# Block-sparse attention and an MLP mixer in one kernel: channel mixing paced over the next batch's attention, gates of the later pairs in fp16 parts

## The chip, the cores and the metric

One core of a Trainium2 chip runs the whole kernel. Five engines work at the same time, each through its own list of instructions in order, and semaphores tie the lists together: TensorE (PE in the profile; its weight loads are PEld), VectorE (DVE), ScalarE (ACT), GpSimd (POOL) and SyncE (SP, which issues transfers here). Matmuls write to PSUM, which is small and is handed out in tiles. The metric is device time in microseconds (us).

## The reference

Inputs are q, k and v of shape (4 batches, 8 heads, 768 positions, 64 wide) and four weight matrices, all float32. The first half is attention in which each query sees only some blocks of 64 keys:

```python
k_rep = k.reshape(B, H, n_blocks, block, D).mean(axis=3)
gate_scores = np.einsum('bhsd,bhnd->bhsn', q, k_rep)
causal = pos[:, None] // block >= np.arange(n_blocks)[None, :]
gate_scores = np.where(causal, gate_scores, -1000000000.0)
top_idx = np.argsort(gate_scores, axis=-1)[..., -top_k:]      # top_k = 3
# a query sees its 3 best blocks and its own, and no later position
scores = scale * np.matmul(q, k.transpose(0, 1, 3, 2))
...
return np.matmul(attn, v).astype(np.float32)
```

The second half takes the attention's output as x (4, 768, 512), mixes over positions and then over channels:

```python
xt = x.transpose(0, 2, 1)
h = np.maximum(xt @ w_tok1, 0.0) @ w_tok2        # 768 -> 256 -> 768
u = x + h.transpose(0, 2, 1)
h2 = np.maximum(u @ w_ch1, 0.0) @ w_ch2          # 512 -> 1536 -> 512
return (u + h2).astype(np.float32)
```

## The kernel before

**Work.** Two heads of one batch make a pair; there are 16 pairs, 4 to a batch, and pair i belongs to batch i // 4. For each pair the kernel

- loads k and q (SyncE) and turns them with fp32 transposes into PSUM (`transposes`, L333), copies them out in fp32 on ScalarE (`evac_t`, L342) and casts each head's half to fp16 on GpSimd (`cast`, L348, into the tiles KA and Q);
- makes the gates: sums each key block (`ksum`, L356), places the two heads' sums in a small fp32 matrix (`kcopy`, L364), multiplies with q in fp32 (`gate`, L374: five matmuls of 24 columns, each recorded as two), adds the causal bias (`gm`, L382), takes the best eight of 12 (`top`, L391), compares with the third (`below`, L398), turns it into a bias (`bias`, L406), transposes that (`mask`, L417) and copies it into spare rows of Q (`put_mask`, L425), so that the score matmul itself adds the block mask;
- computes the scores transposed (keys on the partitions) in three groups for each head (`scores`, L439), the exponential of each group (`expo`, L452), and sets the wrong half of the diagonal blocks to zero: for pair 0 by an added matmul with a triangle (L443, `i < TRI`), for the others by a multiplication on VectorE (`diag`, L458);
- multiplies with v (`av`, L468, 21 matmuls of 65 columns for a head, whose last column gives the sum) and normalises (`recip`, `norm`, L476 and L487).

Token mixing of a batch (`tok1`, `umix`, `uadd`) follows its four pairs; batch 0 does it in quarters as its pairs come. u is turned by TensorE for batch 0 (`utr`, `uput`) and through DRAM by SyncE for the others (`store_u`, `turn_u`). The first half of channel mixing is `ch1` (L580, 24 groups of four matmuls) with a relu after each (`relu2`: the 512-column groups on ScalarE, L590; the 256-column groups on VectorE, L592). The second half is a 2x2-block product done with seven block products instead of eight (`prod`, L644), in three rounds j, each with four operand sums on VectorE (`hsum`), three copies out of PSUM on ScalarE (`keep`, L652), and output sums on VectorE and GpSimd (`vsum`, `oput`, `vu` L666, `psum` L684, `osum` L689).

**Order.** `plan` (L69) sets the order of all instructions before the program is built. Every step is an `Op` with an engine, an assumed duration, the steps it needs, a priority (low goes first) and the buffers it takes; for each engine `plan` takes, among the steps that could start within 60 ns of the earliest one, that of the lowest priority. The priorities are due times: pair i's scores have 10 i and up, its preparation 10 (i - 1) (10 (i - 2.5) for the first four). Batch b's channel mixing has 1000 (b + 1) and up, token mixing of batches 1 to 3 has 960 less: with these, channel mixing goes only where no attention can. Buffers come in rings (`RINGS`): two PSUM tiles `big` of two banks for transposes and scores, three single banks `bank` for gates, masks, token and channel mixing; once all scores are done, channel mixing may take `big` as well.

**Start.** Sixty matmuls on zeros keep TensorE running until the first data is there (`dummy`, L710). The weights are loaded by GpSimd's queue, each after a given cast (`WAIT`).

Of the kernel before, what the change touches and what calls it, by code (L numbers as in the profile page):

```python
# [31 lines left out]
TRI = 1  # L32
EARLY = 1
UVIA = 1
LEAD = 960.0
WARM, COLD, WARM_END = 120, 20, 17000.0
IDLE = 1e9
WAIT = [("kt", 3, 1), ("kt", 3, 1), ("qt", 3, 1), ("qt", 3, 1), ("qt", 4, 1), ("qt", 4, 1),
# [3 lines left out]
class Op:  # L42


    __slots__ = ("eng", "occ", "rec", "deps", "prio", "fn", "takes", "start", "size", "both")

    def __init__(self, eng, occ, rec, deps, prio, fn, takes=(), size=0):
        self.eng, self.occ, self.rec, self.prio, self.fn = eng, occ, rec, prio, fn
        self.deps = [d for d in deps if d is not None]
        self.takes = takes  # L50
        self.size = size
        self.start = None
        self.both = False

# [14 lines left out]
def plan(ops, rings, near=60.0):  # L69
# [10 lines left out]
    for op in ops:  # L80
        n = 0
        for d in op.deps:
            users.setdefault(id(d), []).append(op)
            n += 1
        waiting[id(op)] = n
        if n == 0:
            ready[op.eng].append(op)
# [16 lines left out]
    while left:  # L104
# [7 lines left out]
        for e, cand in ready.items():  # L112
# [7 lines left out]
            for op in cand:  # L120
                t = free[e]
                for d in op.deps:
                    t = max(t, finish(d, e))
                if op.both:
                    t = max(t, free["POOL"]) if t >= pool_from else t
                elif e == "POOL" and both_from <= t < both_to:
                    t = both_to
                ok = True
                for buf in op.takes:
# [10 lines left out]
                    buf.slot = first[1:]  # L140
                if ok:
                    lst.append((t, op))
            if not lst:
                continue
            t0 = min(t for t, _ in lst)
            pick = min((x for x in lst if x[0] <= t0 + near), key=lambda x: (x[1].prio, x[0]))
# [3 lines left out]
        t, op = best  # L150
# [30 lines left out]
        ready[op.eng].remove(op)  # L181
        order.append(op)
        left -= 1
        for u in users.get(id(op), []):
            waiting[id(u)] -= 1
            if waiting[id(u)] == 0:
                ready[u.eng].append(u)
# [4 lines left out]
def kernel(  # L192
# [20 lines left out]
    scale = 1.0 / (D ** 0.5)  # L213
    MASKV = -30000.0
# [8 lines left out]
    RINGS = dict(big=2, bank=3, av=1, ql=3, kl=3, v32=2, qt=2, kt=2, gs=2, e0=3, e1=3, e2=3, rc=2,  # L223
                 x16=2, h1=1, u=2, uT=2, h2=1, ob=3, s1=2, s3=2, s4=1, f32=6)
# [24 lines left out]
    ks2 = [sp.tile([128, 2 * NB], FP, tag=f"ks{r}", name=f"ks{r}") for r in range(R)]  # L249
    bn16 = [sp.tile([128, NJ, 2, 64], F16, tag=f"bn{r}", name=f"bn{r}") for r in range(2)]  # L250
# [22 lines left out]
    def act(cols, deps, prio, fn, takes=()):  # L273
        return op("ACT", 70 + cols * 0.833, 173 + cols * 0.833, deps, prio, fn, takes)

# [60 lines left out]
    def evac_t(t32, i):  # L336
        def f():
            name = "qt" if t32 == "ql" else "kt"
            t = sb(name, [128, S], FP, f"{name}_{i}")
            T[name, i] = t  # L340
            p = T["tr", t32, i]
            nc.scalar.copy(out=t, in_=p[:, 0:S])  # L342
        return f

    def cast(dst, name, i, x):
        def f():
            lo = 64 * x
            nc.gpsimd.tensor_copy(out=dst[i % R][x][lo:lo + 64, :], in_=T[name, i][lo:lo + 64, :])  # L348
        return f
# [9 lines left out]
    def kcopy(i):  # L359
        def f():  # L360
            kst = T["kst", i]
            r = i % R
            for lo, c in ((64, 0), (0, NB)):
                nc.vector.tensor_reduce(out=ks2[r][lo:lo + 64, c:c + NB],  # L364
                                        in_=kst[lo:lo + 64, :].rearrange("p (n o) -> p n o", o=1),
                                        axis=AX.X, op=ALU.add)
        return f

    def gate(i):
        def f():  # L370
            g = ps("bank", [128, GJ, 2 * NB], "gps")
            T["gps", i] = g
            for j in range(GJ):
                nc.tensor.matmul(out=g[:, j, :], lhsT=T["qt", i][:, 128 * j + 128:128 * j + 256],  # L374
                                 rhs=ks2[i % R], start=True, stop=True)
        return f

    def gm(i):
        def f():
            t = sp.tile([128, GJ, 2 * NB], FP, tag="gm", bufs=2, name=f"gm_{i}")  # L380
            T["gm", i] = t
            nc.vector.tensor_tensor(out=t, in0=T["gps", i], in1=gbias, op=ALU.add)  # L382
        return f

    def top(i):
        def f():
            t = sp.tile([128, GJ, 2, 8], FP, tag="m8", bufs=2, name=f"m8_{i}")
            T["m8", i] = t
            for j in range(GJ):
                for x in range(2):  # L390
                    nc.vector.max(out=t[:, j, x, :], in_=T["gm", i][:, j, NB * x:NB * x + NB])  # L391
        return f

    def below(i):
        def f():
            t = sp.tile([128, GJ, 2 * NB], FP, tag="lt", bufs=2, name=f"lt_{i}")
            T["lt", i] = t
            nc.vector.tensor_tensor(  # L398
                out=t.rearrange("p j (x n) -> p j x n", n=NB),
                in0=T["gm", i].rearrange("p j (x n) -> p j x n", n=NB),  # L400
                in1=T["m8", i][:, :, :, 2:3].broadcast_to([128, GJ, 2, NB]), op=ALU.is_lt)
        return f

    def bias(i):
        def f():
            nc.vector.scalar_tensor_tensor(  # L406
                out=bn16[i % 2][:, 1:NJ, :, 0:NB],
                in0=T["lt", i].rearrange("p j (x n) -> p j x n", n=NB), scalar=MASKV,
# [3 lines left out]
    def mask(i):  # L412
        def f():
            p = ps("bank", [128, 128 * GJ], "bps", F16)
            T["bps", i] = p
            for j in range(GJ):
                nc.tensor.transpose(out=p[:, 128 * j:128 * j + 128],  # L417
                                    in_=bn16[i % 2][:, j + 1, :, :].rearrange("p x n -> p (x n)"),
# [3 lines left out]
    def put_mask(i, x):  # L422
        def f():
            lo = 64 if x == 0 else 0
            nc.vector.tensor_copy(out=QA[i % R][x][lo:lo + NB, 128:S], in_=T["bps", i][lo:lo + NB, :])  # L425
# [65 lines left out]

    def tok1(b, t):
# [10 lines left out]
    def relu1(b, t):  # L503
        return lambda: nc.scalar.activation(out=T["h1", b][:, t, :], in_=T["tok1", b, t], func=AF.Relu)
# [29 lines left out]
    def relu1c(b, c):  # L534
        return lambda: nc.scalar.activation(out=T["h1", b][:, :, 128 * c:128 * c + 128], in_=T["tok1", b, c], func=AF.Relu)
# [29 lines left out]
    def uput(b, cc):  # L565
        def f():
            if cc == 0:
                T["uT", b] = sb("uT", [128, NCC, S], F16, f"uT_{b}")
            nc.vector.tensor_copy(out=T["uT", b][:, cc, :], in_=T["utps", b, cc])
# [14 lines left out]
    def relu2(b, fc, n):  # L584
        def f():
            a, e = CH[n]
            if fc == 0 and ("h2", b) not in T:
                T["h2", b] = sb("h2", [128, NFC, S], F16, f"h2_{b}")
            if n == 0:
                nc.scalar.activation(out=T["h2", b][:, fc, a:e], in_=T["c1", b, fc, n], func=AF.Relu)  # L590
            else:
                nc.vector.tensor_scalar(out=T["h2", b][:, fc, a:e], in0=T["c1", b, fc, n], scalar1=0.0,  # L592
                                        scalar2=None, op0=ALU.max)
        return f

    def ch2(b, j, part, lo, hi):
        def f():
            if part == 0:
                T["c2", b, j, lo] = ps("bank", [128, hi - lo], "c2")
            for fc in range(4 * part, 4 * part + 4):  # L600
                nc.tensor.matmul(out=T["c2", b, j, lo], lhsT=T["h2", b][:, fc, 128 * j:128 * j + 128],
                                 rhs=wc2_16[:, fc, lo:hi], start=(fc == 0), stop=(fc == NFC - 1))
# [11 lines left out]
    def halves(b, j):  # L614
        h2 = T["h2", b]
        c1, c2 = slice(128 * j, 128 * j + 128), slice(384 + 128 * j, 512 + 128 * j)
        return h2[:, 0:HF, c1], h2[:, HF:NFC, c1], h2[:, 0:HF, c2], h2[:, HF:NFC, c2]
# [30 lines left out]
    def keep(b, j, key):  # L648
        def f():
            t = sb("f32", [128, 256], FP, f"p{key}_{b}_{j}")  # L650
            T["p" + key, b, j] = t
            nc.scalar.copy(out=t, in_=T["c2" + key, b, j])  # L652
# [77 lines left out]
    for i in range(NP):  # L730
# [9 lines left out]
        for t32, src, off in (("kl", k, 0), ("ql", q, 0.1)):  # L740
# [5 lines left out]
            name = "kt" if t32 == "kl" else "qt"  # L746
            tb = Buf(name)
            if name == "kt" and i < EARLY:
                O["ksum", i] = dve(900, [O["tr", t32, i]], pre + 1, ksum(i))
                big.users.append(O["ksum", i])  # L750
            O[name, i] = act(768, [O["tr", t32, i]] + ([O["ksum", i]] if name == "kt" and i < EARLY else []),
                             pre + 0.5 + off, evac_t(t32, i), [tb])
            big.users.append(O[name, i])
            dst = KA if name == "kt" else QA
            for x in range(2):
                O["cast", name, i, x] = op("POOL", 880, 900, [O[name, i]] + zq + last_scores(x), pre + 4 + off,
                                           cast(dst, name, i, x))
                tb.users.append(O["cast", name, i, x])
            if name == "kt":
                if i >= EARLY:  # L760
                    O["ksum", i] = dve(870, [O["kt", i]], pre + 1, ksum(i))
                    tb.users.append(O["ksum", i])
                O["kcopy", i] = dve(200, [O["ksum", i], O.get(("gate", old))], pre + 1, kcopy(i))
            else:
                qb = tb
# [5 lines left out]
        O["gate", i] = pe(1120, [O["kcopy", i], O["qt", i]], pre + 2, gate(i), [gb])  # L771
        qb.users.append(O["gate", i])
        gs = Buf("gs")
        O["gm", i] = dve(200, [O["gate", i]], pre + 3, gm(i), [gs])
        gb.users.append(O["gm", i])
        O["top", i] = dve(720, [O["gm", i]], pre + 3, top(i))
        O["lt", i] = dve(200, [O["top", i]], pre + 3, below(i))
        O["bias", i] = dve(195, [O["lt", i], O.get(("mask", i - 2))], pre + 3, bias(i), both=True)
# [3 lines left out]
        for x in range(2):  # L782
            O["put", i, x] = dve(410, [O["mask", i]] + zq + last_scores(x), pre + 4, put_mask(i, x))
# [35 lines left out]
    for b in range(B):  # L819
        fill = 1000.0 * (b + 1)  # L820
        mix = fill - LEAD if b else fill
        early = -1.0
# [199 lines left out]
```

## Time and profile before

| | us |
|---|---|
| median of 3 runs (271.99 to 275.36) | 272.19 |
| the profiled execution | 271.2 |
| its span, first to last instruction | 269.4 |
| TensorE busy | 254.9 (95%) |
| VectorE busy | 187.1 (69%) |
| ScalarE busy | 155.1 (58%) |
| GpSimd busy | 129.3 (48%) |

Times inside the profile start at the span's beginning. "Busy" is the union of an engine's records; records of neighbouring instructions can overlap. A line number names the line of the kernel that issued an instruction, and line numbers of the changed kernel differ from those of the kernel before. In the profile's rows, `out<-in` gives the program's tile names without numbers, then the shapes, then how often; after the bar come busy us and the mean duration in ns. Two rows of operations that the change removes or moves, as the view of groups by shape gives them: the fp32 gate matmuls take 20.0 us of records (160 of them, mean 267 ns), the diagonal multiplication 18.3 us (30, mean 611 ns).

### The profile page before, as it was taken

The numbers are of one execution on the slowest core, as the hardware profiler recorded it, in microseconds if no ns is written. First come the engines' busy times: TensorE is split into PE (matmuls) and PEld (weight loads), VectorE is DVE, ScalarE is ACT, GpSimd is POOL, SyncE is SP. The second block draws the span as 40 slices with busy tenths as digits, with TensorE's granted clock in tenths as the row PEclk, the third lists the DMA queues.
The fourth block names the chain that finished last, engine by engine and source line by source line (L and its number), as shares of the span: only waits on it lengthen the run. The fifth ranks groups of instructions, "written<-read, shape, count | busy, mean of one in ns | idle before, by whom it ended". The sixth has DMA issues, their size and how long they took to land.

```text
span 269.4 us, 6752 instructions
## 1 busy us (share of the span) xinstructions
PE 254.9 (95%) x2640; PEld 198.3 (74%) x2640; DVE 187.1 (69%) x574; ACT 155.1 (58%) x224; POOL 129.3 (48%) x171
## 2 busy tenths in 40 slices
PE   8798889999998999999999999999999999999992
PEld 5687678887776878778788887656775558866881
DVE  4468768889799978659997974418953459544861
ACT  2357798697888788977678872442224432244220
POOL 8678907478418563544826155000890006910384
PEclk9999999999999999999999999999999999999998
DMA  8999999999999944747048213000581004920033
GB/s 174 199 210 226 170 208 226 207 220 192 231 205 229 195 102 98 157 102 135 2 136 100 82 42 116 2 0 0 195 213 62 2 0 157 230 86 2 0 119 117
DMA packets 94240, 34.69 MB, mean 129 GB/s; under 512 B 85568, under 2 KB 90584, under 8 KB 94208
## 3 DMA queue, kind: packets, MB, share of 16 engines
q1 hardware_dynamic: 90128, 29.89, 51.9%
q0 software_dynamic: 3360, 4.11, 9.0%
q8 instruction: 21, 0.34, 0.6%
q10 hardware_dynamic: 720, 0.25, 0.5%
q14 instruction: 11, 0.09, 0.1%
HBM read 27.17 MB, written 8.65 MB: 133 GB/s over the span
## 4 chain that ended last, share of the span: by engine, by line
PE 66%; DVE 17%; DMA 6%; POOL 5%; issue 2%; ACT 1%; SPq 1%; POOLq 0%; DVEq 0%; ACTq 0%
PE c L580 21%; PE c L644 14%; PE sps L439 9%; PE aps L468 5%; PE gps L374 5%; DMA ql<-in_q_dram 4%; PE tok L499 3%; DMA wc<-in_moe_w_ch_dram 3%; POOL vu L666 2%; PE tql L333 2%; DVE u L519 2%; DVE Q L425 2%; PE tkl L333 2%; DVE e L458 2%; PE ups L511 2%
## 5 line engine op out<-in xcount | busy, mean ns | idle before, releaser
L452 ACT ACTIVATE e<-sps 128x768 f16<-128x768 f32 (+2 forms) x96 | 85.4, 920 | 15.3 <-PE sps L439 14.1
L580 PE MATMUL c<-uT,wc 128*128 128x256 f16 (+1 forms) x384 | 66.8, 326 | 0.0
L580 PEld LDWEIGHTS <-wc 128*128 128x128 f16 x384 | 37.0, 98 | 22.5
L439 PE MATMUL sps<-Q,KA 128*128 128x128 f16 (+3 forms) x384 | 50.5, 259 | 2.6 <-ACT e L452 2.5
L666 POOL TENSOR_TENSOR vu<-v,u 128x256 f32<-128x256 f32 x36 | 28.6, 819 | 34.7 <-DVE v L659 34.3
L590 ACT ACTIVATE h<-c 128x512 f16<-128x512 f32 x48 | 28.7, 597 | 27.2 <-PE c L580 27.0
L592 DVE TENSOR_SCALAR h<-c 128x256 f16<-128x256 f32 x48 | 20.2, 421 | 31.8 <-PE c L580 31.6
L348 POOL CAST KA<-kt 64x768 f16<-64x768 f32 x32 | 27.0, 844 | 28.8 <-ACT kt L342 27.7
L439 PEld LDWEIGHTS <-KA 128*128 128x128 f16 x384 | 29.4, 100 | 14.4 <-issue 2.2
L348 POOL CAST Q<-qt 64x768 f16<-64x768 f32 x32 | 27.6, 862 | 9.8 <-ACT qt L342 8.5
L644 PEld LDWEIGHTS <-h 128*128 128x128 f16 x288 | 27.7, 98 | 5.1 <-DVE h L629 1.3
L684 POOL TENSOR_TENSOR pc<-pc,pd 128x256 f32<-128x256 f32 x12 | 9.1, 760 | 41.2 <-ACT pd L652 41.2
L468 PE MATMUL aps<-V,e 128*128 128x65 f16 x672 | 26.7, 193 | 0.2 <-ACT e L452 0.2
L468 PEld LDWEIGHTS <-e 128*128 128x128 f16 x672 | 25.2, 98 | 2.0 <-ACT e L452 0.3
L304 POOL CAST V<-v 128x768 f16<-128x768 f32 x16 | 14.6, 913 | 20.6 <-DMA v<-in_v_dram 17.3
L644 PEld LDWEIGHTS <-s 128*128 128x128 f16 x216 | 20.9, 98 | 2.9
L342 ACT COPY kt<-tkl 128x768 f32<-128x768 f32 x16 | 12.8, 800 | 16.2 <-PE tkl L333 9.9
L374 PEld LDWEIGHTS gps<-ks,qt 128*128 128x128 f32 x160 | 19.2, 192 | 2.9 <-DVE ks L364 1.1
L374 PE MATMUL gps<-ks,qt 128*128 128x24 f32 x160 | 20.0, 267 | 1.3 <-ACT qt L342 0.5
L458 DVE TENSOR_TENSOR e<-e,m 128x768 f16<-128x768 f16 x30 | 18.3, 611 | 3.0 <-ACT e L452 2.8
L644 PE MATMUL c<-t,h 128*128 128x256 f16 x144 | 19.4, 273 | 0.6 <-DVE h L629 0.6
L644 PE MATMUL c<-wc,h 128*128 128x256 f16 x144 | 19.6, 273 | 0.0
(73 smaller groups left out, 372.1 us busy)
## 6 DMA issues: line engine op xcount, KB each, us to landing
kl<-in_k_dram SPq DMA_DIRECT2D x32, 192.0 KB, 4.7
ql<-in_q_dram SPq DMA_DIRECT2D x32, 192.0 KB, 4.5
v<-in_v_dram SPq DMA_DIRECT2D x16, 384.0 KB, 5.4
out_dram<-ob SPq DMA_DIRECT2D x24, 256.0 KB, 2.3
wc<-in_moe_w_ch_dram POOLq DMA_DIRECT2D x8, 384.0 KB, 7.4
uscr<-u SPq DMA_DIRECT2D x3, 768.0 KB, 3.7
w<-in_moe_w_tok_dram POOLq DMA_DIRECT2D x2, 384.0 KB, 7.2
KA<-indc POOLq DMA_DIRECT2D x2, 72.0 KB, 4.6
```

What stands on the lines that cost most here:

```text
L304: nc.gpsimd.tensor_copy(out=V16[i % (R + 1)][:, :, :, 0:D], in_=T["v32", i])
L348: nc.gpsimd.tensor_copy(out=dst[i % R][x][lo:lo + 64, :], in_=T[name, i][lo:lo + 64, :])
L374: nc.tensor.matmul(out=g[:, j, :], lhsT=T["qt", i][:, 128 * j + 128:128 * j + 256], rhs=ks2[i % R], start=True, stop=True)
L439: nc.tensor.matmul(out=p[:, off + a:off + a + n], lhsT=KA[i % R][x][:, 128 * kk:128 * kk + 128], rhs=QA[i % R][x][:, q0 + a:q0 + a + n], s ...
L452: nc.scalar.activation(out=e[:, 0:width], in_=T["sps", i, x, g][:, 0:width], func=AF.Exp, scale=scale)
L458: nc.vector.tensor_tensor(out=d, in0=d, in1=m0.broadcast_to([128, NJ, 128]), op=ALU.mult)
L468: nc.tensor.matmul(out=p[:, jq, :], lhsT=T["e", i, x, g][:, o:o + 128], rhs=V16[i % (R + 1)][:, x, kk, :], start=(kk == 0), stop=(kk == jq))
L580: nc.tensor.matmul(out=p, lhsT=wc1_16[:, cc, 128 * fc:128 * fc + 128], rhs=T["uT", b][:, cc, a:e], start=(cc == 0), stop=(cc == NCC - 1))
L590: nc.scalar.activation(out=T["h2", b][:, fc, a:e], in_=T["c1", b, fc, n], func=AF.Relu)
L592: nc.vector.tensor_scalar(out=T["h2", b][:, fc, a:e], in0=T["c1", b, fc, n], scalar1=0.0, scalar2=None, op0=ALU.max)
L644: nc.tensor.matmul(out=T["c2" + key, b, j], lhsT=x[:, fc, :], rhs=y[:, fc, :], start=first and fc == 0, stop=fc == HF - 1, skip_group_chec ...
L666: nc.gpsimd.tensor_tensor(out=t, in0=T["v", b, j], in1=T["u", b][:, j + 3 * row, 256 * col:256 * col + 256], op=ALU.add)
```

## The change

- **Pacing.** Batch b's token mixing gets the priority 40 (b + 1), and its channel mixing is spread from there over the next batch's 40 units of attention, 22 units late (`PACE`, `SKEW`, `pace`). Batch 0's token mixing gets 10 (c + 1).
- **Gates.** Keys and queries are scaled by 8 when they are copied out. Pairs 0 to 3 keep the fp32 gates, but their bias sum and comparison are written in place in PSUM. Pairs 4 to 15 copy q out as fp16 (`qh`) and compute the remainder as a second fp16 tile (`qr`, on VectorE, read from the transposes in PSUM); the key sums are split likewise into two fp16 parts by four small GpSimd instructions (`split_k`); the gate is ten fp16 matmuls of 48 columns; the bias sum becomes two instructions. q's place in Q is then a copy of fp16 as pairs (64x384 fp32 elements) instead of a cast.
- **Triangles.** `TRI` goes from 1 to 4: pairs 0 to 3 mask their diagonals with TensorE.
- **Either engine.** Copies and relus out of PSUM may go to ScalarE or to VectorE (`either`); `plan` takes the one that it expects to be done first.
- **Buffers and planner.** h2 is split in two halves with a buffer each, the rings s1 and s3 go from 2 to 1, kt and qt share a ring of three, and before 15 us the planner's choice looks 250 ns ahead instead of 60. Unused functions go.

```diff
-TRI = 1
+TRI = 4
-LEAD = 960.0
+HEAD = 15000.0
+INBANK = 4
+SPLIT = 4
+PACE, SKEW = 40.0, 22.0
...
+    def either(cols, slow, deps, prio, fn, takes=()):
+        o = act(cols, deps, prio, fn, takes)
+        o.alt = ("DVE", slow, slow + 84)
+        return o
...
+    def rest_q(i):
+        def f():
+            t = sb("qr", [128, S - 128], F16, f"qr_{i}")
+            T["qr", i] = t
+            nc.vector.scalar_tensor_tensor(out=t, in0=T["tr", "ql", i][:, 128:S], scalar=UP, in1=T["qh", i][:, 128:S],
+                                           op0=ALU.mult, op1=ALU.subtract)
...
+    def split_k(i):
...
+                    hi, lo = t[rows, 1 - x, 0, :], t[rows, 1 - x, 1, :]
+                    if c == 0:
+                        nc.gpsimd.tensor_copy(out=hi, in_=kst[rows, :])
+                    else:
+                        nc.gpsimd.tensor_tensor(out=lo, in0=kst[rows, :], in1=hi, op=ALU.subtract)
...
+    def gate_parts(i):
...
+                for n, t in enumerate((T["qh", i][:, 128 * j + 128:128 * j + 256], T["qr", i][:, 128 * j:128 * j + 128])):
+                    nc.tensor.matmul(out=g[:, j].rearrange("p x c n -> p (x c n)"), lhsT=t,
+                                     rhs=kp[i % 2].rearrange("p x c n -> p (x c n)"), start=(n == 0), stop=(n == 1))
...
+            nc.vector.tensor_tensor(out=cut(t), in0=g[:, :, :, 1, :], in1=cut(gbias), op=ALU.add)
+            nc.vector.tensor_tensor(out=cut(t), in0=g[:, :, :, 0, :], in1=cut(t), op=ALU.add)
...
-        fill = 1000.0 * (b + 1)
-        mix = fill - LEAD if b else fill
+        mix = PACE * (b + 1)
+        def pace(us):
+            return mix + SKEW + PACE * us / 30.0
...
-                                        fill + 20 + 2 * k + n, ch1(b, fc, n, bk), [bk])
+                                        pace(1.3 * k + 0.87 * n), ch1(b, fc, n, bk), [bk])
...
-            at = fill + 50 + 10 * j
+            at = pace(15.6 + 4.62 * j)
```

## The prediction

> **What bounds the kernel now.** I read the page first, then the windows of three stages, then PE's waits, then the timeline for the price of single steps.
>
> The page, busy time and slices:
>
> ```profile
> PE 254.9 (95%) x2640; PEld 198.3 (74%) x2640; DVE 187.1 (69%) x574; ACT 155.1 (58%) x224; POOL 129.3 (48%) x171
> ...
> PE   8798889999998999999999999999999999999992
> ...
> PEclk9999999999999999999999999999999999999998
> ```
>
> The windows before the first channel matmul (0 to 65 us), with attention and channel mixing together (to 162), with channel mixing alone (to 264.1), and the tail; columns as in the first line:
>
> ```profile
> core 0: us, PE busy (x) PEld busy (x) DVE busy (x) ACT busy (x) POOL busy (x), PEclk, DMA share, GB/s
> 0.00:65.00 65.00, 57.76 (x730) 49.28 (x731) 46.70 (x180) 42.84 (x54) 43.53 (x67) 1.00 1.14 205
> 65.00:162.00 97.00, 95.35 (x1174) 77.02 (x1172) 81.61 (x272) 77.54 (x102) 47.66 (x56) 1.00 0.66 131
> 162.00:264.10 102.10, 101.48 (x740) 71.95 (x739) 57.99 (x123) 34.69 (x69) 36.15 (x48) 1.00 0.26 77
> 264.10:269.40 5.30, 0.29 (x3) 0.01 (x1) 0.75 (x2) 0.00 (x0) 1.98 (x3) 0.84 0.39 148
> ```
>
> TensorE sets the end: full from 65 us on at a granted clock of 1.00, while VectorE, the next, stands at 84% (81.6 of 97.0) at its worst. A busy PE need not be at its peak, so I took the distance from one matmul's start to the next; its median by shape is 216 ns for 512 columns, 109 for 256, 56 for 128, 32 for the 65 of the value product, and 112 for each of the two halves that an fp32 gate matmul is recorded as. Number times median is PE's work; what is over is lost. 0 to 65: work 46.4, warm-up matmuls 6.5, lost 11.0, first start 1.1. 65 to 162: work 94.4, lost 2.6. 162 to 264.1: work 101.0, lost 1.1. Tail 5.3. Together 269.4, the span: 241.8 of work and 27.6 of everything else. So from 65 us on the kernel costs what PE's matmuls cost, and their order hardly matters. PE's longest waits, all early (what waited for what, total us, times, longest):
>
> ```profile
> PE sps L439 <- ACT e L452: 2.5, 5, 0.7
> PE bps L417 <- DVE bn L406: 1.8, 4, 1.1
> PE tql L333 <- DMA ql<-in_q_dram: 1.7, 2, 1.0
> ```
>
> **The change, part by part.**
>
> *Gates in fp16 parts.* The timeline has the price of an fp32 gate: it starts at 110.31, the next work at 111.40, 1.09 us for one pair.
>
> ```profile
> 102.36 0.83 PE L468 MATMUL aps<-V,e 128*128 128x65 f16 x21
> 103.03 0.54 PE L439 MATMUL sps<-Q,KA 128*128 128x512 f16 x3
> ...
> 110.31 1.25 PE L374 MATMUL gps<-ks,qt 128*128 128x24 f32 x10
> 111.40 0.93 PE L439 MATMUL sps<-Q,KA 128*128 128x128 f16 x9
> ```
>
> Pairs 4 to 15 get ten fp16 matmuls of 48 columns instead. The nearest row is the value product: 21 of 65 columns from 102.36 to 103.03, 32 ns each, so 0.32 us; the far end is the 56 ns of 128 columns, 0.56. I take 0.32, the nearer width: 12 x (1.09 - 0.32) = 9.2 us off PE; at 56 ns 6.4. A loss needs more than 109 ns each, and no fp16 row of under 256 columns has that.
>
> The Trainium skill, TensorE: Matmul & The Clock Gate, "Wait — 56ns, not 53.3ns?", gives a floor of about 25 ns between starts however few the columns. The value product stands above it at 32; by the floor the saving would be an estimated 10.1 us.
>
> *TensorE triangles for pairs 1 to 3.* 3 pairs x 2 heads x 6 matmuls of 56 ns add 2.0 us to PE; six VectorE masks of 0.61 us go (3.7).
>
> *Pacing.* It adds no matmul: the same 384 of channel mixing's first half and 504 of its second stand elsewhere. In the changed order the last value product is followed by 52.6 us of PE work (now 102), the first channel matmul comes after 40.2 (now 46.4), and 141.7 lie between. So attention is stretched over channel mixing instead of running ahead of it. What must hold is that the other engines keep below PE in that middle. By the counts of the changed order, at these rows, VectorE has 138.6 us of records there; records overlap (over the whole run 213 summed against 187 busy), so some 122, or 86% of PE's 141.7. That is the 84% at which 65 to 162 lost 2.6 in 97. I take that rate: 3.8 us lost. ScalarE has 108 of 142, below today's 80%; GpSimd under 80.
>
> *The other engines, whole run.* VectorE gains 12 remainders of q (640 columns; nearest the 128x512 sum at 0.68 and the 128x768 reduction at 0.93; I take 0.75: 9.0), 12 second gate sums (0.28: 3.4), five wide relus (3.4), five kept products (2.1), three small relus (1.3). It loses 24 key copies of 0.16 (3.8), the masks (3.7), 15 narrow relus of 0.42 (6.3) and seven mask copies of 0.48 (3.4): up 2.0, to 189. ScalarE rises 4.5, to 160: 15 narrow relus 5.8 and seven mask copies 4.8 against wide relus, kept products and small relus of 6.1. GpSimd loses 24 casts of 0.86, gains 24 copies of 64x384 (0.41, as the memsets, to 0.86) and 48 operations of 64x12. Nothing so small but the 0.11 us constants ran there; a 64x384 memset is 0.41: 5.3 to 19.7 in all, and I take 0.2 each, 9.6, as 12 columns lie nearer to the small end: level. All this lies beside PE and costs nothing while PE stays full. If the cover goes, a late 64x12 on GpSimd holds the gate, and the gate holds every matmul behind it in PE's order.
>
> *The head.* SyncE's 79 transfers keep their order, and warm-up matmuls fall from 60 to 50 but only fill gaps. For pairs 0 to 3 gate sums and comparisons now stay in PSUM. Today one comparison takes 0.79 and the bias after it 0.85 while GpSimd casts (23.08 to 24.79), against 0.28 and 0.27 when it doesn't (12.14, 13.74):
>
> ```profile
> 23.25 0.79 DVE L398 TENSOR_TENSOR lt<-gm,m 128x120 f32<-128x120 f32 x1
> 24.08 0.85 DVE L406 SCALAR_TENSOR_TENSOR bn<-lt,own 128x120 f16<-128x120 f32 x1
> ```
>
> The chain that ended last runs through both, and through another bias of 0.84 at 31.44: 0.5 + 0.6 + 0.6 = 1.7 us over the undisturbed rows, of which I take 1.0, because pairs 0 to 3 then wait for ScalarE. Against it GpSimd's first arithmetic instruction moves from batch 0's first output sum to pair 4's key split, where no channel work is ready, and takes its pool-configuration instructions along. Today they stand at 142.89, and the instruction behind them starts at 144.84:
>
> ```profile
> 144.84 1.05 POOL L666 TENSOR_TENSOR vu<-v,u 128x256 f32<-128x256 f32 x1 [1.90 <-DVE v L659]
> ```
>
> So they hold at most 1.9 us, and perhaps nothing, since v came at 144.7. I take 0.5 (what the trace shows is a wait for v): the head gains 0.5, bounds +1 to -3.
>
> The Trainium skill, GPSIMD Engine Reference, "Instruction dispatch", speaks against this change: a freshly loaded kernel's first call pays about 6 us of loading. The row allows 1.9 unless the load began earlier, unseen. By the page the head would lose an estimated 5.5 more, and 264.1 would be 269.6.
>
> *The end.* Batch 3's u goes through DRAM behind 21 products (13.8 us); today 20 cover it, and the first channel matmul follows at 234.84 without a gap. Single buffers for two operand sums leave four products (2.6 us) to cover two sums (1.4). Nothing is taken; the tail's operations are the same, 5.3.
>
> **The sum.** Work 241.8 - 9.2 + 2.0 = 234.6. The rest: before the first channel matmul 18.6 now, 18.1 then; middle 3.8; end 0.6 (1.1 x 52.6/102); tail 5.3. Span 262.4, against 269.4. The profiled execution took 271.2, 1.8 over its span: 264.2. The median of the runs, 272.19, is 1.0 above that execution, which I leave out: **264.1 us**.
>
> **Rivals.**
> - *The head opens up*, 259.5: without triangles and port clashes half of the 6.3 us lost from 20 to 65 goes, and the middle loses under 2. For: ScalarE and VectorE end those waits. Against: so do loads, whose order stands.
> - *The middle starves PE*, 269.5: a third of it (47 us) loses at the rate of 20 to 65, 0.139 instead of 0.027, 5.3 more. For: q's PSUM tile is now held through a second reader, on VectorE, and three banks serve channel products beside gates and masks. Against: 133 to 162 already interleaves all of it and loses 0.3.
> - *The gate's new link on GpSimd comes late*, 282: the split queues behind casts and output sums in batches 1 to 3, the fp16 gate (L446) waits for it at the head of PE's order, and the channel work meant as filler stands behind it. At 1.5 us for each of 12 pairs, 18 over forecast. Over 2% slower from 1.13 us a pair. For: order alone decides, and GpSimd gets 12.9 us of work where PE has 14.3 around pairs 14 and 15. Against: prefetch a whole pair ahead, some 12 us (141.7 for 12 pairs), for about 7 us of chain (the rows from key copy to mask copy, with a split of 0.8).
> - *The gates get no cheaper*, 273.4: switching weights, not columns, is the price, and ten loads stay ten. Against: the value product changes weights every 32 ns.
>
> **Chances.** Forecast 0.55 (260.5 to 267.5), head 0.12, starved middle 0.20, late gates 0.08, dear gates 0.05. The range 258.5 to 273.5 takes in all but late gates and some edges, 0.15. 2% of 272.19 is 5.4 us, about what a measurement of this kernel can tell from no change. Faster by that (below 266.7): most of the forecast, the head, a little of the middle, 0.63. Within: 0.28. Slower: late gates and edges, 0.09.
>
> **What would show it.** fp16 gates: starts some 32 ns apart, PE's work near 234.6. Middle: PE at 97% or more between first channel matmul and last value product, the latter near 204 us. Wrong if PE shows waits for kp or qr, if VectorE passes 90% there, or if the first channel matmul starts after 60 us.

## The result, and the profile after

| | before | after |
|---|---|---|
| median of the runs, us | 272.09 (4 runs) | 263.16 (4 runs) |
| after / before, 95% interval | | 0.9677 (0.9647 to 0.9707) |
| profiled execution, us | 271.2 | 263.1 |
| span, us | 269.4 | 261.3 |

Four kernels of the experiments (fp32 gates, fixed engines, remainder twice planned, batch 0 last) each had one run in a slower state, which the medians and ratios below leave out.

The forecast of 264.1 us was 0.9 above the measured time. The page of the changed kernel, busy time and slices:

```profile
PE 246.6 (94%) x2666; PEld 189.1 (72%) x2666; DVE 191.2 (73%) x561; ACT 159.4 (61%) x233; POOL 131.8 (50%) x219
...
PE   7699889989999999999999999999999999999991
...
PEclk9999999999999999999999999999999999999999
```

The windows before the first channel matmul, up to the last value product, channel mixing alone, and the tail:

```profile
core 0: us, PE busy (x) PEld busy (x) DVE busy (x) ACT busy (x) POOL busy (x), PEclk, DMA share, GB/s
0.00:57.60 57.60, 50.09 (x661) 42.53 (x661) 36.15 (x140) 36.87 (x45) 35.84 (x66) 1.00 1.18 206
57.60:201.90 144.30, 142.85 (x1605) 107.68 (x1604) 121.08 (x355) 104.52 (x151) 72.16 (x124) 1.00 0.58 125
201.90:256.60 54.70, 53.62 (x408) 38.84 (x404) 33.86 (x68) 18.01 (x39) 22.39 (x29) 1.00 0.25 78
256.60:261.30 4.70, 0.00 (x0) 0.00 (x0) 0.12 (x1) 0.00 (x0) 1.42 (x3) 0.88 0.29 112
```

PE is as full as before, over 8 us less. The middle has grown from 97 to 144 us, and VectorE's share in it is still 84% (121.1 of 144.3). Taken apart as the prediction did it, by the distance from one matmul's start to the next (us; each column is one profiled execution):

| | before | after | after minus before |
|---|---|---|---|
| work of the matmuls | 241.9 | 233.4 | -8.5 |
| lost between them | 14.6 | 15.6 | +1.0 |
| warm-up, first start, tail | 12.9 | 12.3 | -0.6 |
| span | 269.4 | 261.3 | -8.1 |

"Lost" takes in the gaps between the warm-up matmuls, 4.0 us before and 3.8 after; "warm-up" is the work of these matmuls. In this account the 8 us are PE's work, and the work is the gates. One fp16-part gate in PE's timeline runs from 46.95 to 47.21:

```profile
46.95 0.19 PE L446 MATMUL gps<-kp,qh 128*128 128x48 f16 x1
46.98 0.18 PE L446 MATMUL gps<-kp,qr 128*128 128x48 f16 x1
47.01 0.18 PE L446 MATMUL gps<-kp,qh 128*128 128x48 f16 x1
...
47.21 0.22 PE L525 MATMUL sps<-Q,KA 128*128 128x128 f16 x1
```

Starts are 25 ns apart (median of all 120). Ten of them take 0.25 us where the fp32 gate took 1.12: 12 x 0.87 = 10.4 us off. The 36 added triangles put 2.0 back.

PE's waits after: none is longer than 1.4 us, and the two that stood first before have shrunk from 2.5 to 1.0 (exponential) and from 1.8 to 0.8 (bias).

```profile
PE tql L361 <- DMA ql<-in_q_dram: 2.0, 2, 1.4
PE tql L361 <- ACT kt L366: 1.1, 2, 0.8
PE warm L795 <- DVE warm L1069: 1.1, 1, 1.1
PE sps L525 <- ACT e L538: 1.0, 2, 0.7
PE bps L503 <- DVE bn L493: 0.8, 3, 0.4
...
PE sps L525 <- DVE qr L388: 0.3, 1, 0.3
```

### The profile page after: what moved, and what is told of

The parts are those of the page before. It is cut to its first block, busy times and chain, and to the rows that moved or that the text cites. A ratio compares the mean times of both kernels' runs of the same rounds, so it can differ in the third digit from the quotient of the medians.

```text
span 261.3 us, 6831 instructions
## 1 busy us (share of the span) xinstructions
PE 246.6 (94%) x2666; PEld 189.1 (72%) x2666; DVE 191.2 (73%) x561; ACT 159.4 (61%) x233; POOL 131.8 (50%) x219
## 4 chain that ended last, share of the span: by engine, by line
PE 63%; DVE 13%; DMA 10%; POOL 6%; issue 3%; ACT 2%; SPq 1%; POOLq 0%; DVEq 0%; ACTq 0%
PE c L678 23%; PE c L729 12%; PE sps L525 9%; PE aps L554 5%; DMA v<-in_v_dram 4%; PE tok L597 3%; DMA w<-in_moe_w_tok_dram 3%; PE tql L361 2%; PE ups L609 2%; PE tkl L361 2%; POOL vu L751 2%; DMA ql<-in_q_dram 2%; DVE u L617 1%; DMA out_dram<-ob 1%; PE bps L503 1%
## 5 line engine op out<-in xcount | busy, mean ns | idle before, releaser
L769 POOL TENSOR_TENSOR pc<-pc,pd 128x256 f32<-128x256 f32 x12 | 10.1, 841 | 30.9 <-ACT pd L586 30.7
L580 ACT ACTIVATE h2a<-c 128x512 f16<-128x512 f32 (+1 forms) x30 | 16.1, 540 | 10.8 <-PE c L678 10.4
L580 ACT ACTIVATE h2b<-c 128x512 f16<-128x512 f32 (+1 forms) x28 | 15.1, 544 | 11.5 <-PE c L678 11.3
L366 ACT ACTIVATE kt<-tkl 128x768 f32<-128x768 f32 x16 | 13.0, 810 | 11.5 <-PE tkl L361 6.5
L729 PE MATMUL c<-wc,s 128*128 128x256 f16 x144 | 19.6, 272 | 0.0
L582 DVE TENSOR_SCALAR h2b<-c 128x256 f16<-128x256 f32 (+1 forms) x20 | 9.2, 459 | 12.3 <-PE c L678 12.2
L573 DVE TENSOR_TENSOR x<-aps,rc 128x384 f16<-128x384 f32 x32 | 17.7, 552 | 0.7
L401 POOL COPY Q<-qh 64x384 f32<-64x384 f32 x24 | 14.6, 607 | 3.7 <-ACT qh L381 2.6
L361 PE MATMUL tql<-id,ql 128*128 128x128 f32 x96 | 13.4, 275 | 3.1 <-DMA ql<-in_q_dram 2.0
L729 PEld LDWEIGHTS <-h2a 128*128 128x128 f16 x144 | 13.5, 98 | 3.2 <-DVE h2a L714 0.9
L468 DVE TENSOR_REDUCE kst<-kt 128x12 f32<-128x768 f32 x15 | 14.0, 934 | 2.2 <-ACT kt L366 2.2
```

Of the source, the lines that this page charges most:

```text
L361: nc.tensor.transpose(out=p[:, 128 * j:128 * j + 128], in_=t[:, j, :], identity=ident32)
L401: nc.gpsimd.tensor_copy(out=QA[i % R][x][lo:lo + 64, :].bitcast(FP), in_=T["qh", i][lo:lo + 64, :].bitcast(FP))
L468: nc.vector.tensor_reduce(out=kst, in_=kt.rearrange("p (n w) -> p n w", w=64), axis=AX.X, op=ALU.add)
L573: nc.vector.tensor_tensor(out=T["x16", b][:, :, 64 * hh:64 * hh + 64], in0=T["aps", i, x][:, :, 0:64], in1=T["rc", i, x].broadcast_to([128 ...
L580: e.activation(out=out, in_=src, func=AF.Relu)
L729: nc.tensor.matmul(out=T["c2" + key, b, j], lhsT=x[:, fc, :], rhs=y[:, fc, :], start=first and fc == 0, stop=fc == HF - 1, skip_group_chec ...
```

## The experiments

The theory that the prediction stood on: from the first channel matmul on, the time is PE's work, and order and other engines add little (theory PE). Its rivals: that pacing and the free choice of engines brought the gain, and that the new links on GpSimd and VectorE cost something. "Lost" below is from the profiled execution of that run; the changed kernel lost 15.6 us. The ratios were taken beside other runs of the kernel before, whose medians lay between 271.4 and 272.1 us, so a ratio times such a median can differ by some tenths of a us from the median in the second column.

| run | median us | ratio to the kernel before (95%) | work | lost |
|---|---|---|---|---|
| the change | 263.16 | 0.9677 (0.9647 to 0.9707) | 233.4 | 15.6 |
| fp32 gates | 272.56 | 1.0039 (1.0009 to 1.0070) | 243.9 | 14.7 |
| one pair of triangles | 263.92 | 0.9725 (0.9649 to 0.9802) | 231.4 | 17.1 |
| unpaced | 263.96 | 0.9736 (0.9651 to 0.9822) | 233.4 | 16.3 |
| fixed engines | 264.65 | 0.9744 (0.9666 to 0.9821) | 233.4 | 16.7 |
| gates alone | 266.73 | 0.9808 (0.9733 to 0.9883) | 231.4 | 22.8 |
| gate four times | 270.38 | 0.9942 (0.9903 to 0.9981) | 242.4 | 14.6 |
| split twice | 268.57 | 0.9893 (0.9806 to 0.9979) | 233.4 | 20.2 |
| remainder twice | 268.20 | 0.9860 (0.9795 to 0.9925) | 233.4 | 20.3 |
| split twice, planned | 267.64 | 0.9849 (0.9808 to 0.9890) | 233.4 | 20.2 |
| remainder twice, planned | 266.00 | 0.9765 (0.9704 to 0.9825) | 233.4 | 19.4 |
| batch 0 last | 262.33 | 0.9665 (0.9625 to 0.9704) | 232.1 | 17.8 |
| two fp32 pairs | 263.03 | 0.9685 (0.9649 to 0.9721) | 230.4 | 20.1 |

### fp32 gates: the gate part undone

```diff
-SPLIT = 4
+SPLIT = 16
```

(with the ring of key sums as before, and the bias sum out of PSUM from pair 4 on)

> The changed kernel (263.2 us) with all 16 pairs' gates in fp32 as before; everything else of the change stays. Theory PE: from the first channel matmul on, the end is set by the sum of the matmuls' times, so 12 pairs x (10 x 0.112 - 10 x 0.025) = 10.4 us come back: 273.6, 272 to 275. Rival relief: it was the spread of work over the engines and the pacing that brought the gain, and fp32 gates free VectorE of 12 remainders and 12 second sums (some 13 us): 266 or less.

Measured 272.56, in theory PE's range. Against the change that is 0.0362 of 271.4, 9.8 us, where theory PE said 10.4; the work rose by 10.5 and the loss fell by 0.9. The rival (266 or less) is out. The kernel with everything but the fp16 gates is no faster than the kernel before: without the gates nothing of the gain is left.

### One pair of triangles

```diff
-TRI = 4
+TRI = 1
```

> The changed kernel with TensorE triangles for pair 0 alone; pairs 1 to 3 are masked by VectorE as before. Theory PE: 36 matmuls of 56 ns go, 2.0 us: 261.2, 260.5 to 262. Rival head: the triangles take six VectorE masks of 0.61 us out of the crowded first 65 us and pay for themselves there: 263 to 266 without them.

263.92 is in the rival's range and not to be told from the change; theory PE's range (up to 262) isn't reached. The work fell by the 2.0 us, and the loss rose by 1.5. So the triangles on PE about pay for themselves; that they bring more isn't shown.

### Unpaced

```diff
-        mix = PACE * (b + 1)
+        fill = 1000.0 * (b + 1)
+        mix = fill - 960.0 if b else fill
...
-            return mix + SKEW + PACE * us / 30.0
+            return fill + 20 + us
```

(and the older steps of the due times within a batch)

> The changed kernel with the old priorities of token and channel mixing (only where no attention can go). Theory PE: the same matmuls in another order, within 1 us: 262.2 to 264.2, with the last value product some 40 us earlier. Rival pacing: spreading attention keeps the other engines below TensorE and is worth over 2%: 268.5 or more without it.

263.96: theory PE. The last value product ends near 169 us instead of 202, so the order is quite another, and the time is the same within what the runs tell. The middle loses more (6.0 us of 112 against 3.6 of 144), the stretch from 20 us to the first channel matmul less (3.9 against 5.8).

### Fixed engines

```diff
     def either(cols, slow, deps, prio, fn, takes=(), dv=False):
-        o = act(cols, deps, prio, fn, takes)
-        o.alt = ("DVE", slow, slow + 84)
-        return o
+        if dv:
+            return dve(slow, deps, prio, lambda: fn(nc.vector), takes)
+        return act(cols, deps, prio, lambda: fn(nc.scalar), takes)
```

> The changed kernel with copies and relus bound to the engines that they had before (mask copies, 256-column relus of channel mixing and batch 0's copies of turned u on VectorE, the rest on ScalarE). Theory PE: nothing on TensorE changes, 262.2 to 264.7, more being lost in the first 65 us at most. Rival relief: the choice of engine keeps VectorE and ScalarE below TensorE while attention and channel mixing share them: 266 or more without it.

264.65, at the upper end of theory PE's range, and its interval reaches the change's. The profiled execution lost 1.1 more, with 6.0 in the middle against 3.6. By itself this part isn't shown to matter.

### Gates alone

All of the last three edits together, and the planner's longer look ahead at the start and the gate sums in PSUM undone as well (the smaller rings s1, s3 and kt with qt stay as in the change):

```diff
-TRI = 4
+TRI = 1
-HEAD = 15000.0
+HEAD = 0.0
-INBANK = 4
+INBANK = 0
```

> The kernel before with the gate part of the change alone: fp16-part gates for pairs 4 to 15 (with the scaling by 8 and the split h2 buffers), but one pair with triangles, old priorities, fixed engines, no longer look ahead at the start, no gate sums in PSUM. Theory PE: 12 pairs x (10 x 0.112 - 10 x 0.025) = 10.4 us off TensorE and no triangles added: 272.1 - 10.4 = 261.7, 260.5 to 263.5, as fast as the whole change or faster. Rival whole: the gates need the pacing and the free choice of engines to carry VectorE's and GpSimd's new work: 266 or more.

266.73: theory PE is 5 us too low here, and the time lies in the rival's range. The work is 231.4, 2.0 below the change's, and the loss is 22.8. PE's waits in it:

```profile
PE sps L526 <- ACT e L539: 2.1, 6, 0.7
PE aps L555 <- DVE x L574: 2.0, 2, 1.6
PE tql L361 <- DMA ql<-in_q_dram: 1.8, 2, 1.4
PE c L679 <- DMA uT<-uscr: 1.2, 1, 1.2
PE bps L504 <- DVE bn L494: 1.1, 1, 1.1
```

They are of many kinds: exponentials, a normalisation, a bias, batch 3's u that came 1.2 us late. In the middle, between the first channel matmul and the last value product, VectorE is busy for 90% of the time, where the change has 84%, and 7.0 us are lost against 3.6:

```profile
63.20:165.80 102.60, 98.83 (x1260) 76.05 (x1259) 92.85 (x295) 82.83 (x111) 58.11 (x100) 1.00 0.64 134
```

Whether VectorE's share is the cause isn't shown: between 133 and 162 us the kernel before has it at 88% (25.55 of 29.00) and hardly loses anything. The four kernels, as ratios to the kernel before:

| | rest as before | rest as in the change |
|---|---|---|
| fp32 gates in all pairs | 1 | 1.0039 |
| gates in fp16 parts from pair 4 | 0.9808 | 0.9677 |

The rest of the change is worth nothing with the old gates, and 0.9808 - 0.9677 = 1.3%, 3.6 us, with the new ones, though PE does 2.0 us more in it. The difference of the two, 1.7%, stands against an uncertainty of some 0.9%, worked out from the three intervals. Which of its parts brings the 3.6 us stays open. Triangles, pacing and choice of engine, undone singly, read 0.5, 0.6 and 0.7%, none of them clear of nothing; they add up to 1.7%, so that these parts simply add is not excluded. The look ahead and the gate sums in PSUM were not undone singly, and the rings nowhere. (This profiled execution took 269.2, 2.5 over its kernel's median, partly for a drop of the clock that is told at the end, so its 22.8 is somewhat high.)

### Gate four times: PE's own price

```diff
-            for j in range(GJ):
+            for j in [j for j in range(GJ) for _ in range(4)]:
                 for n, t in enumerate((T["qh", i][:, 128 * j + 128:128 * j + 256], ...
```

> The changed kernel in the same order of steps, each fp16 gate matmul issued four times (40 of 25 ns for a pair, 1.0 us, about what the fp32 gate takes). The values stay. Theory PE: 12 x 30 x 0.025 = 9.0 us more: 272.2, 271 to 273. Rival cover: TensorE has slack beside attention, and part of 9 us goes into gaps: under 269.

270.38, between the two ranges: 9.0 us of work cost 7.2, and the loss fell from 15.6 to 14.6. With the result of the fp32 gates, a microsecond of PE is worth 0.8 to 0.94 of time. In both, the loss between matmuls fell by about 1 us: a PE with more to do waited a little less.

### Split twice, and remainder twice: the price of the other links

```diff
-            for c in range(2):
+            for c in (0, 1, 0, 1):
```

> The changed kernel in the same order, the key split on GpSimd done twice (8 small instructions of 0.24 us instead of 4, about 0.95 us more ahead of each gate, 11.5 us of GpSimd in all). Theory PE: the prefetch hides it from pair 6 on; 263.2 to 265, pairs 4 and 5 alone paying. Rival late gates: the split sits on the path to the gate and holds TensorE's order: 12 x 0.95 = 11, 274.

```diff
+            for _ in range(2):
                 nc.vector.scalar_tensor_tensor(out=t, in0=T["tr", "ql", i][:, 128:S], scalar=UP, ...
```

> The changed kernel in the same order, the remainder of q on VectorE computed twice (0.8 us more for each of 12 pairs, 9.8 us of VectorE, and the PSUM tile of the transposes held as much longer). Theory PE: VectorE stands at some 85% of TensorE's time in the middle and this lifts it to some 92%: 263.2 to 266. Rival starved middle: VectorE is next to bound there and gives all of it on: 271 or more.

268.57 and 268.20 lie above theory PE's ranges and below the rivals'. GpSimd was busy for 142.9 us instead of 131.8, and these 11.1 us cost 5.4; 9.8 us of added VectorE records cost 5.0. That is about half; with the ratios' intervals, 0.3 to 0.7. PE's longest waits with the split twice:

```profile
PE gps L446 <- POOL kp L415: 1.8, 3, 0.7
PE gps L446 <- ACT e L538: 1.1, 1, 1.1
```

And the middle of that run:

```profile
58.40:206.50 148.10, 143.56 (x1607) 107.90 (x1605) 120.58 (x355) 105.38 (x151) 82.33 (x165) 1.00 0.56 121
```

GpSimd is busy for 82.3 of 148.1 us, so it has room; PE stands at the gate because the parts come late, not because GpSimd is full. From the first channel matmul on, PE stood before six of the ten gates for 0.1 to 1.3 us, 3.6 in all; in the change it stood before none of them. With the remainder twice VectorE is at 127.0 of 147.7, 86%, and the waits are small and spread (bias 1.4, exponential 1.8).

### The same, planned

Was it that the order had been laid out for shorter steps?

```diff
-                    O["kcopy", i] = op("POOL", 1080, 1120, ...
+                    O["kcopy", i] = op("POOL", 2040, 2080, ...
```

> The key split on GpSimd done twice as before (e7: 268.6), but the planner is told that it takes 2.04 us instead of 1.08 and orders all steps anew. Theory order: the engines have room (GpSimd 83 of 144 us busy in the middle), and what e7 lost was a fixed order that reached the gate before its key parts; with the later gate planned for it is back at 263.2 to 265. Rival room: the chain to the mask has no slack of 0.95 us whatever the order, 267.5 to 269.

```diff
-                O["qr", i] = dve(740, [O["qh", i]], pre + 2, rest_q(i), [rb])
+                O["qr", i] = dve(1480, [O["qh", i]], pre + 2, rest_q(i), [rb])
```

> The remainder of q on VectorE computed twice (e8: 268.2), with the planner told 1.48 us instead of 0.74. Theory order: 263.5 to 265.5, since VectorE has some 130 of 144 us in the middle. Rival room: VectorE is so near to TensorE there that its work counts about half whatever the order, 267 to 269.

267.64 and 266.00: planning for the longer step gives back 0.9 and 2.2 us, the first within what the runs can tell, the second just at its edge. For the split, theory order is out: 267.64 lies in the rival's range, and PE still waits for kp three times, 2.0 us in all. For the remainder neither holds: 266.00 is between the two ranges, so the order was part of its price. There PE's longest wait after the start is one of 1.9 us before a score matmul for qr: the remainder still reads the transposes from PSUM, and scores and transposes share the two `big` tiles. In the two orders tried for each, the slack on the way to a mask was too small for the longer step in some pairs.

### Two attempts at a better kernel

```diff
-TRI = 4
+TRI = 2
...
-                at = 10.0 * (c + 1)
+                at = 1000.0 + c
...
-uadds[cc], mix + 0.1 * cc, utr(b, cc)
+uadds[cc], 1000.6 + cc, utr(b, cc)
```

> The changed kernel with batch 0's token mixing at its old priority (only where attention leaves room; the pacing of all else stays) and triangles for pairs 0 and 1 instead of 0 to 3. Theory: TensorE's work falls by 24 x 0.056 = 1.3 us, and the first stretch, which lost 3.9 us from 20 us to the first channel matmul in the unpaced kernel, loses less than the 5.8 of the changed one: 260 to 262.5. Rival: the freed time in the first 58 us goes to other waits (loads, VectorE's masks), 263 to 264.5.

And besides that:

```diff
-INBANK = 4
-SPLIT = 4
+INBANK = 2
+SPLIT = 2
```

> As the run with batch 0's token mixing last and two pairs with triangles, with the fp16-part gates from pair 2 on instead of pair 4. Theory: two more pairs x (1.12 - 0.25) = 1.7 us less of TensorE: 1.7 below that run, 258.5 to 261. Rival: in the first 58 us TensorE's work is not what sets the pace, and two more remainders and splits lengthen the chain to the masks there: equal to that run or above.

262.33 and 263.03: neither can be told from the change. The first lies in its theory's range, but its profiled execution shows 1.3 us less of work and no gain in the stretch that the theory named (5.6 us lost there against 5.8). That execution (263.88) also holds a wait of 2.3 us that the last section tells of. The second lies above its theory's range (258.5 to 261), where its rival had it. In it, PE's work is 3.0 us below the change's, and the loss 4.5 above, 9.3 of it between 20 us and the first channel matmul against 5.8: up to there PE's work does not set the pace, as its rival had it.

## Why the prediction was right, point by point

- **What bounds it.** Right for the change as a whole: span and work fell together (8.1 and 8.5). Unpaced bears out "their order hardly matters" for the changed kernel. But that the other engines' work "costs nothing while PE stays full" is too strong, and the gates alone show it: with the old order, engines, triangles and start, only 5.2 of the 10.4 us come through.
- **The gate's term** was mis-sized: 0.32 us for ten matmuls, from the 65-column value product, against 0.25 measured; 9.2 us forecast, 10.4 found on PE and 9.8 in time. The floor of about 25 ns that the Trainium skill gives (TensorE: Matmul & The Clock Gate, "Wait — 56ns, not 53.3ns?") is what 48 columns take here; the estimate that went by it, 10.1, was the nearer one.
- **Triangles**: 2.0 of work as forecast, but in time nothing is seen, since six VectorE masks went with them.
- **The sum.** Work 234.6 forecast, 233.4 found. Loss of the middle 3.8 and 3.6. Before the first channel matmul, apart from work, 18.1 and 17.5; that matmul at 58.3 and 57.6 us. End 0.6 and 1.1, tail 5.3 and 5.7. Span 262.4 and 261.3, and 1.8 over it in both. The work was 1.2 too high, the head 0.6 and the middle 0.2; end and tail were 0.9 too low together. That the sum came out to within 0.9 is in part luck: the same reckoning by PE's work was 5.0 us too low for the gates alone.
- **The middle's cover.** The share of VectorE, 86% forecast, is 84%. But "the prefetch a whole pair ahead" was no cover of 5 us: 0.95 more of GpSimd ahead of each gate cost 0.45 of time per pair. The rival of late gates named the right place, but nothing of the kind happens in the change as it is: PE shows no wait for kp there. It shows one for qr, of 0.3 us; the prediction had called such a wait a sign of being wrong, and this one is too short to count.
- **The head.** Bias and comparison in PSUM are no longer held up while GpSimd casts. In the timeline of the change:

```profile
21.82 1.71 POOL L395 CAST Q<-qt 64x768 f16<-64x768 f32 x2
22.42 0.29 DVE L487 TENSOR_TENSOR gps<-gps,m 128x120 f32<-128x120 f32 x1
22.75 0.28 DVE L493 SCALAR_TENSOR_TENSOR bn<-gps,own 128x120 f16<-128x120 f32 x1
```

  against 0.79 and 0.85 before. The 0.5 charged for GpSimd's pool configuration was 0.09 at most: it now stands at 44.7 us, between

```profile
44.27 0.44 POOL L413 CAST kp<-kst 64x12 f16<-64x12 f32 x2
44.80 0.48 POOL L415 TENSOR_TENSOR kp<-kst,kp 64x12 f16<-64x12 f32 x2
```

  with 0.09 us from the end of the one to the start of the other. The some 6 us that the Trainium skill gives for a freshly loaded kernel's first call (GPSIMD Engine Reference, "Instruction dispatch") are not there in this case. Had they been charged, the forecast would have been 269.6, 6.4 above the measured time.
- **Pacing** was forecast to add nothing by itself, and undone by itself it changes nothing that can be told (263.96).

## What to carry to other kernels

When one engine is full, price a change by that engine's start-to-start times, and then price what the change adds to the others: here a microsecond of PE was worth 0.8 to 0.94, and a microsecond ahead of the masks on VectorE or GpSimd about half, though those engines were busy for 86% and 56%. The second price holds for those two experiments and is no general one. For the gates alone it comes near: 12 x (0.82 remainder + 0.28 second sum - 0.32 key copies) = 9.4 us more on VectorE, half of it 4.7, off the 10.4 leaves 5.7, and 5.2 was measured. But the fp32 gates take the same 9.4 us off VectorE again, and by this price they should have cost 5.7 us; they cost 9.8. What a part is worth depends on what stands beside it: the rest of this change is worth nothing without the new gates and 3.6 us with them. So test the main part alone and the rest without it, and not only the parts singly.

## What the runs showed of the hardware

In three of the profiled executions a short gap on PE came with 3.4 us at half the granted clock. In that of "batch 0 last", VectorE computes sums of just landed weights ahead of a remainder; a score matmul waits 2.3 us for it:

```profile
70.10 0.60 PE L678 MATMUL c<-uT,wc 128*128 128x256 f16 x4
73.01 1.01 PE L525 MATMUL sps<-Q,KA 128*128 128x512 f16 x3 [2.30 <-DVE qr L388]
```

and the windows of that stretch show the clock:

```profile
72.00:73.00 1.00, 0.00 (x0) 0.00 (x0) 1.00 (x3) 0.00 (x0) 0.65 (x1) 0.92 1.10 235
73.00:74.00 1.00, 0.99 (x7) 0.55 (x7) 0.96 (x3) 0.00 (x0) 0.18 (x1) 0.50 1.17 229
74.00:75.00 1.00, 1.00 (x15) 0.65 (x12) 0.62 (x3) 0.89 (x1) 0.00 (x0) 0.50 1.24 225
75.00:76.00 1.00, 1.00 (x5) 0.40 (x3) 0.96 (x12) 0.88 (x2) 0.00 (x0) 0.50 1.32 233
76.00:77.00 1.00, 1.00 (x11) 0.63 (x9) 1.00 (x3) 0.51 (x2) 0.00 (x0) 0.88 0.87 149
```

Ten gate matmuls in it stand 40 ns apart instead of 25. The half clock lasts 3.4 us. By start-to-start distances the matmuls begun between 73.0 and 76.45 us are 1.9 us of work and took 3.5, so the drop cost some 1.5 us on top of the wait. In "gates alone" two waits of 0.73 and 1.07 us within 2.5 us (30.1 to 32.6) came with the same 3.4 us at half clock, and in "two fp32 pairs" two of 0.67 and 0.96 us (the second from 11.5 to 12.4).

The length of a gap does not decide it alone. Single gaps of 1.9 us ("remainder twice, planned", 78.3 to 80.1) and 1.7 us ("fixed engines", 75.1 to 76.9) were followed by no drop, and in "batch 0 last" gaps of 0.70 and 0.96 us passed at full clock at nearly the same places as in "two fp32 pairs". No run here shows what decides. In the profiled execution of the change no such drop is recorded before the tail.
